# Layer scale on one core: laying rows out in HBM in contiguous blocks of 4, 60 and 64 per partition

## The chip, the core and the metric

The kernel runs on one core of a Trainium2 chip. The metric is the device time of one execution in microseconds; the median of three runs stands for a kernel. A profile is one more execution, recorded by the hardware profiler.

## What is computed

```python
B, S, D = 1024, 16, 512
# x, y: (B, S, D) bf16; gamma: (D,) bf16
def reference(x, y, gamma):
    return x + gamma * y
```

There are 1024 x 16 = 16384 rows of 512 values. A row is 1 KB in bf16. Each of x, y and the output has 16.78 MB, so 50.33 MB cross between HBM and SBUF. Every row is treated alike, so it does not matter to the result which row lies in which SBUF partition, as long as x, y and the output use one and the same assignment.

## The kernel before

**Layout.** The 16384 rows are spread over 128 partitions, 128 rows each. In HBM a partition's 128 rows are neighbours (`"(p n) d -> p n d"`, L52 to L54), so row r of one partition lies 128 KB from row r of the next. All of y stays in SBUF (`y_sb`, 128 rows of each partition). `x_sb` has room for 75 rows only: the second half of x is loaded over rows that have been used. The output is computed in place in `y_sb`.

**Transfers.** Two lists say what each DMA queue issues and in which order. `SP` (L10) has six loads, each written as (tensor, first row, end row) and for x also the row of `x_sb` where it goes: y rows 0 to 4, y 4 to 64, x 0 to 64, y 64 to 128, x 64 to 117, x 117 to 128. `ACT` (L11) has gamma and two stores, rows 0 to 64 and 64 to 128. The function `ring` walks such a list: y loads are issued at L116, x loads at L113, stores at L119, gamma at L110. `EARLY = (2, 0)` puts the first two loads of SP ahead of the barrier at the program's beginning. A transfer of r rows is moved as 128 packets of r KB, one for each partition, which the 16 DMA engines share, eight each.

**Waits.** A load of x into occupied rows waits for the additions that used them (`frees`), a store for the additions of its rows, both through `s_add`. The first store also waits for `s_go`, which TensorE raises (L135 to L137) once x rows 64 to 117 have landed. Each load has its own semaphore, and VectorE takes it ahead of the first operation on these rows.

**Compute.** The rows of a partition are worked on in pieces of 53, 11, 53 and 11 rows (`PIECES`). `DVE` (L18) gives the order: multiply pieces 0 and 1 by gamma (L156), add x to them (L165), then the same for pieces 2 and 3. Gamma is spread over the partitions once, by a matmul with a row of ones (L130) and a copy (L132).

The lines that set the layout:

```python
xv = xf.rearrange("(p n) d -> p n d", p=P)
yv = yf.rearrange("(p n) d -> p n d", p=P)
ov = of.rearrange("(p n) d -> p n d", p=P)
```

Of the kernel before, what the change touches and what calls it, by code (L numbers as in the profile page):

```python
# [3 lines left out]


PIECES = [53, 11, 53, 11]

SP = [('y', 0, 4), ('y', 4, 64), ('x', 0, 64, 0), ('y', 64, 128), ('x', 64, 117, 0), ('x', 117, 128, 64)]  # L10
ACT = [('g',), ('s', 0, 64), ('s', 64, 128)]  # L11

EARLY = (2, 0)


RELEASE = ('x', 64, 117, 0)

DVE = [('m', 0), ('m', 1), ('a', 0), ('a', 1), ('m', 2), ('m', 3), ('a', 2), ('a', 3)]  # L18
MULT, ADD = mybir.AluOpType.mult, mybir.AluOpType.add


def _take(sem, n, eng):


    return eng.wait_ge(sem, n).then_inc(sem, -n)  # L25


def kernel(
# [10 lines left out]
    P = nc.NUM_PARTITIONS  # L39
# [3 lines left out]
    xf = x.flatten_outer_dims()  # L43
    yf = y.flatten_outer_dims()
    of = out.flatten_outer_dims()
    N, D = xf.shape
    rows = N // P
    n = len(PIECES)
    assert sum(PIECES) == rows
    starts = [sum(PIECES[:c]) for c in range(n + 1)]  # L50
    dt = xf.dtype
    xv = xf.rearrange("(p n) d -> p n d", p=P)  # L52
    yv = yf.rearrange("(p n) d -> p n d", p=P)
    ov = of.rearrange("(p n) d -> p n d", p=P)  # L54

    gamma_row = nc.alloc_sbuf_tensor("gamma_row", [1, D], dt).ap()
    ones_row = nc.alloc_sbuf_tensor("ones_row", [1, P], dt).ap()
# [1 line left out]
    y_sb = nc.alloc_sbuf_tensor("y_sb", [P, rows, D], dt).ap()  # L59
    x_loads = [w for w in SP + ACT if w[0] == "x"]  # L60
    y_loads = [w for w in SP + ACT if w[0] == "y"]
    stores = [w for w in SP + ACT if w[0] == "s"]
    for loads in (x_loads, y_loads, stores):
# [7 lines left out]
    s_load = {w: sem("s_" + "_".join(map(str, w[:2]))) for w in x_loads + y_loads}  # L71
    s_add, s_go, s_rel, s_end, s_out = sem("s_add"), sem("s_go"), sem("s_rel"), sem("s_end"), sem("s_out")
    added = [a for kind, *a in DVE if kind == "a"]
    order = {a[0]: k for k, a in enumerate(added)}

    def meets(a, b, c, d):
        return a < d and c < b

    def pieces_of(a, b):
        return [c for c in range(n) if meets(starts[c], starts[c + 1], a, b)]  # L80

    def x_at(row):
        return next(w[3] + row - w[1] for w in x_loads if w[1] <= row < w[2])

    def frees(w):

        c = set()
        for v in x_loads[: x_loads.index(w)]:
            lo, hi = max(v[3], w[3]), min(v[3] + v[2] - v[1], w[3] + w[2] - w[1])
            if lo < hi:  # L90
                c |= set(pieces_of(v[1] + lo - v[3], v[1] + hi - v[3]))
        return sorted(c)
# [3 lines left out]
    def ring(eng, what, n_early):  # L96

        known, went = 0, False
        for k, w in enumerate(what):
            kind = w[0]  # L100
            need = frees(w) if kind == "x" else pieces_of(w[1], w[2]) + list(w[3:]) if kind == "s" else []
            need = max((order[c] + 1 for c in need), default=0)
            if kind == "s" and not went:
                _take(s_go, 1, eng)
                went = True
            if need > known:
                eng.wait_ge(s_add, need)
                known = need
            if kind == "g":
                i = eng.dma_start(out=gamma_row, in_=gamma.unsqueeze(0)).then_inc(s_gamma, 16)  # L110
            elif kind == "x":
                to = x_sb[:, w[3] : w[3] + w[2] - w[1], :]
                i = eng.dma_start(out=to, in_=xv[:, w[1] : w[2], :]).then_inc(s_load[w], 16)  # L113
            elif kind == "y":
                r = slice(w[1], w[2])
                i = eng.dma_start(out=y_sb[:, r, :], in_=yv[:, r, :]).then_inc(s_load[w], 16)  # L116
            else:
                r = slice(w[1], w[2])
                i = eng.dma_start(out=ov[:, r, :], in_=y_sb[:, r, :]).then_inc(s_out, 16)  # L119
            if k < n_early:  # L120
                early.append(i.ins)

    ring(nc.sync, SP, EARLY[0])
    ring(nc.scalar, ACT, EARLY[1])


# [7 lines left out]

    _take(s_load[RELEASE], 16, nc.tensor)  # L135
    nc.tensor.sem_inc(s_go, 1)
# [4 lines left out]
    def need(loads, c):  # L141
        for w in loads:
            if w not in landed and meets(starts[c], starts[c + 1], w[1], w[2]):
                if w == RELEASE:
                    _take(s_rel, 1, nc.vector)
                else:
                    _take(s_load[w], 16, nc.vector)
                landed.add(w)

    for kind, *args in DVE:  # L150
        c = args[0]
        yt = y_sb[:, starts[c] : starts[c + 1], :]
        if kind == "m":
            need(y_loads, c)
            g = gamma_sb[:, None, :].to_broadcast([P, PIECES[c], D])
            nc.vector.tensor_tensor(out=yt, in0=yt, in1=g, op=MULT).then_inc(s_dve, 1)  # L156
            open_mults += 1
        else:
# [4 lines left out]
            at = x_at(starts[c])  # L163
            xt = x_sb[:, at : at + PIECES[c], :]
            nc.vector.tensor_tensor(out=yt, in0=xt, in1=yt, op=ADD).then_inc(s_add, 1)  # L165
# [44 lines left out]
```

## Time and profile before

| what | value |
|---|---|
| median of 3 runs | 119.99 us (119.95 to 120.16) |
| span of the profiled execution | 118.7 us |
| own time of the profiled execution | not given apart from its span; the median run is 1.29 us above that span |
| VectorE busy | 70.0 us (59%), 10 instructions |
| TensorE busy | 0.6 us, 1 matmul |
| loads, SP's queue (q1) | 864 packets, 33.55 MB, 66.0% of 16 engines' span |
| stores and gamma, ACT's queue (q10) | 290 packets, 16.78 MB, 32.6% |
| one large multiplication or addition (53 rows) | 14.29 us |
| one small one (11 rows) | 3.08 us |

The span runs from the first recorded instruction to the last event of the kernel. Busy times are sums over an engine's instructions. For the queues, the share is the time that their packets took, as a part of 16 engines over the whole span; the two shares together are 98.6%. A packet count includes one small completion write for each DMA engine and transfer.

### The profile page before, as it was taken

How to read it: one execution, taken by the hardware profiler on the slowest of the kernel's cores; microseconds unless marked ns; L12 is line 12 of the kernel's file. 1: busy time of each engine (PE TensorE's matmuls, PEld its weight loads, DVE VectorE, ACT ScalarE, POOL GpSimd, SP SyncE). 2: the span in 40 equal slices, each digit the busy share in tenths (PEclk: the TensorE clock that was granted, in tenths of full speed). 3: DMA queues.
4: the chain of work that ended last, by engine and by line, in shares of the span. 5: the costliest groups of instructions: out<-in, count | busy, mean ns of one | idle time of the engine just before them, and what ended most of it. 6: DMA issues, size and time to landing. Idle time of an engine off the chain costs nothing. (4 is left out here: it accounts for less than half of the span.)

```text
span 118.7 us, 80 instructions
## 1 busy us (share of the span) xinstructions
PE 0.6 (0%) x1; PEld 0.1 (0%) x1; DVE 70.0 (59%) x10; POOL 0.2 (0%) x4
## 2 busy tenths in 40 slices
PE   0001000000000000000000000000000000000000
PEld 0000000000000000000000000000000000000000
DVE  0002000599999299999759999999999910000000
POOL 0000000000000000000000000000000000000000
DMA  8977977998899888998896969498899889988891
GB/s 268 571 332 331 663 331 331 596 464 353 353 486 574 353 353 353 640 420 353 353 585 293 585 293 585 205 634 353 353 596 464 353 353 420 640 353 353 353 663 44
DMA packets 1154, 50.33 MB, mean 424 GB/s; under 512 B 129, under 2 KB 130, under 8 KB 258
## 3 DMA queue, kind: packets, MB, share of 16 engines
q1 hardware_dynamic: 864, 33.55, 66.0%
q10 hardware_dynamic: 290, 16.78, 32.6%
HBM read 33.56 MB, written 16.78 MB: 424 GB/s over the span
## 5 line engine op out<-in xcount | busy, mean ns | idle before, releaser
L156 DVE TENSOR_TENSOR y_sb<-y_sb,gamma_sb 128x27136 bf16<-128x27136 bf16 (+1 forms) x4 | 34.6, 8688 | 12.3 <-DVEq L25 12.3
L165 DVE TENSOR_TENSOR y_sb<-x_sb,y_sb 128x27136 bf16<-128x27136 bf16 (+1 forms) x4 | 34.6, 8689 | 2.3 <-DVEq L25 2.2
L132 DVE CAST gamma_sb<-gamma_ps 128x512 bf16<-128x512 f32 x1 | 0.7, 692 | 8.8 <-DVEq L25 8.8
L127 DVE MEMSET ones_row<- 1x128 bf16 x1 | 0.2, 165 | 2.0 <-PEq L41 2.0
L130 PE MATMUL gamma_ps<-gamma_row,ones_row 1*128 1x512 bf16 x1 | 0.6, 577 | 10.2 <-PEq L25 10.2
L130 PEld LDWEIGHTS gamma_ps<-gamma_row,ones_row 1*128 1x128 bf16 x1 | 0.1, 99 | 10.2 <-issue 10.2
L194 POOL MEMSET const-bfloat16-1.0<- 128x1 bf16 x1 | 0.1, 101 | 0.0
L194 POOL MEMSET const-uint8-127<- 128x1 uint8 x1 | 0.1, 101 | 0.0
L194 POOL MEMSET const-float32-0.0<- 128x1 f32 x1 | 0.1, 98 | 0.2 <-issue 0.2
L194 POOL MEMSET const-float32-1.0<- 128x1 f32 x1 | 0.1, 98 | 0.0
## 6 DMA issues: line engine op xcount, KB each, us to landing
y_sb<-in_y_dram SPq DMA_DIRECT2D x1, 7680.0 KB, 21.4
x_sb<-in_x_dram SPq DMA_DIRECT2D x1, 6784.0 KB, 20.8
x_sb<-in_x_dram SPq DMA_DIRECT2D x1, 1408.0 KB, 23.8
y_sb<-in_y_dram SPq DMA_DIRECT2D x1, 512.0 KB, 3.8
out_dram<-y_sb ACTq DMA_DIRECT2D x2, 22.8
x_sb<-in_x_dram SPq DMA_DIRECT2D x1, 39.3
gamma_row<-in_gamma_dram ACTq DMA_DIRECT2D x1, 1.0 KB
y_sb<-in_y_dram SPq DMA_DIRECT2D x1, 58.3
```

The costliest lines, as they stand in the source:

```text
L127: nc.vector.memset(ones_row, 1.0).then_inc(s_ones, 1)
L130: nc.tensor.matmul(gamma_ps, ones_row, gamma_row, start=True, stop=True).then_inc(s_ps, 1)
L132: nc.vector.tensor_copy(out=gamma_sb, in_=gamma_ps).then_inc(s_dve, 1)
L156: nc.vector.tensor_tensor(out=yt, in0=yt, in1=g, op=MULT).then_inc(s_dve, 1)
L165: nc.vector.tensor_tensor(out=yt, in0=xt, in1=yt, op=ADD).then_inc(s_add, 1)
L194: nc = _bacc.Bacc("TRN2", target_bir_lowering=False, num_devices=1)
```

## The change

The rows are assigned to partitions differently. The 128 rows of a partition are split into blocks of 4, 60 and 64 rows (`BLOCKS`). A block of all partitions together is one contiguous stretch of HBM, and inside it a partition has its 4, 60 or 64 rows as neighbours. A new function `rows_of` gives the piece of a block that a transfer moves; loads and stores use it in place of the three views. A transfer may not cross from one block into another, so x rows 0 to 64 are loaded as 0 to 4 and 4 to 64, and the store of rows 0 to 64 becomes two, rows 4 to 64 first and then rows 0 to 4. The places in SBUF, the pieces of VectorE and their order are kept; the first addition (piece 0, rows 0 to 53) now takes two semaphores of x instead of one.

```diff
+BLOCKS = [4, 60, 64]
+
 PIECES = [53, 11, 53, 11]
...
-SP = [('y', 0, 4), ('y', 4, 64), ('x', 0, 64, 0), ('y', 64, 128), ('x', 64, 117, 0), ('x', 117, 128, 64)]
-ACT = [('g',), ('s', 0, 64), ('s', 64, 128)]
+SP = [
+    ("y", 0, 4),
+    ("y", 4, 64),
+    ("x", 0, 4, 0),
+    ("x", 4, 64, 4),
+    ("y", 64, 128),
+    ("x", 64, 117, 0),
+    ("x", 117, 128, 64),
+]
+ACT = [("g",), ("s", 4, 64), ("s", 0, 4), ("s", 64, 128)]
...
-    xv = xf.rearrange("(p n) d -> p n d", p=P)
-    yv = yf.rearrange("(p n) d -> p n d", p=P)
-    ov = of.rearrange("(p n) d -> p n d", p=P)
+    edges = [sum(BLOCKS[:c]) for c in range(len(BLOCKS) + 1)]
+    assert edges[-1] == rows
+
+    def rows_of(t, a, b):
+
+        c = max(c for c in range(len(BLOCKS)) if edges[c] <= a)
+        assert b <= edges[c + 1]
+        block = t[P * edges[c] : P * edges[c + 1]].rearrange("(p n) d -> p n d", p=P)
+        return block[:, a - edges[c] : b - edges[c], :]
...
-                i = eng.dma_start(out=to, in_=xv[:, w[1] : w[2], :]).then_inc(s_load[w], 16)
+                i = eng.dma_start(out=to, in_=rows_of(xf, w[1], w[2])).then_inc(s_load[w], 16)
...
-                i = eng.dma_start(out=y_sb[:, r, :], in_=yv[:, r, :]).then_inc(s_load[w], 16)
+                i = eng.dma_start(out=y_sb[:, r, :], in_=rows_of(yf, w[1], w[2])).then_inc(s_load[w], 16)
...
-                i = eng.dma_start(out=ov[:, r, :], in_=y_sb[:, r, :]).then_inc(s_out, 16)
+                i = eng.dma_start(out=rows_of(of, w[1], w[2]), in_=y_sb[:, r, :]).then_inc(s_out, 16)
```

More of the change, by code (lines that the diff above doesn't have):

```diff
@@ L3 @@
 from concourse import mybir
+BLOCKS = [4, 60, 64]
 PIECES = [53, 11, 53, 11]
-SP = [('y', 0, 4), ('y', 4, 64), ('x', 0, 64, 0), ('y', 64, 128), ('x', 64, 117, 0), ('x', 117, 128, 64)]
-ACT = [('g',), ('s', 0, 64), ('s', 64, 128)]
+SP = [
[8 more added lines that the diff above has]
+ACT = [("g",), ("s", 4, 64), ("s", 0, 4), ("s", 64, 128)]
 EARLY = (2, 0)
-RELEASE = ('x', 64, 117, 0)
-DVE = [('m', 0), ('m', 1), ('a', 0), ('a', 1), ('m', 2), ('m', 3), ('a', 2), ('a', 3)]
+RELEASE = ("x", 64, 117, 0)
+DVE = [("m", 0), ("m", 1), ("a", 0), ("a", 1), ("m", 2), ("m", 3), ("a", 2), ("a", 3)]
 MULT, ADD = mybir.AluOpType.mult, mybir.AluOpType.add
```

## The prediction

> **What bounds the kernel now.** I read the page first for its busy rows, then its queues, then the DMA-issue timeline, then the DMA view of the first four microseconds. The rows of 40 slices:
>
> ```profile
> DVE  0002000599999299999759999999999910000000
> DMA  8977977998899888998896969498899889988891
> HBM read 33.56 MB, written 16.78 MB: 424 GB/s over the span
> ```
>
> The DMA engines are loaded from the first slice to the last, VectorE is done a fifth before the end, and 50.33 MB in 118.7 us is 424 GB/s. The stretches say whether that leaves anything:
>
> ```profile
> 1.00:2.50 1.50, 0.00 (x0) 0.00 (x0) 0.17 (x1) 0.00 (x0) 1.00 0.95 216
> 2.50:118.40 115.90, 0.58 (x1) 0.10 (x1) 69.87 (x9) 0.00 (x0) 1.00 1.00 431
> ```
>
> The last two columns are DMA share and GB/s: from 2.5 to 118.4 us the engines are busy all the time at 431 GB/s, and only the first 1.5 us of traffic runs at half of it. So the time is bytes over a fixed rate, plus what is lost at the start and at the end. The start, in slices of 0.1 us (a packet's bytes count where it begins):
>
> ```profile
> DMA  0000000000999003029487989599999999000000
> GB/s 0 0 0 0 0 0 0 0 0 0 287 164 205 0 0 41 0 123 328 205 328 328 369 369 492 246 451 1024 1516 2704 860 1884 1311 1843 0 0 0 0 0 0
> DMA packets 160, 1.51 MB, mean 377 GB/s; under 512 B 16, under 2 KB 16, under 8 KB 144
> ```
>
> Sixteen 4 KB packets begin between 1.0 and 1.3 us, and then hardly any begins for 0.5 us: the engines stand in their first packet of y rows 0 to 4. The packet records give the sizes: a 4 KB packet later takes 159 ns, but of the first 16 two take 0.20 and 0.26 us, two 0.33 and 0.55 us, and the other twelve 0.62 to 1.16 us. Over the 128 packets of this transfer the sum is 30.6 us instead of 128 x 0.159 = 20.4, so 10.3 us over 16 engines, **0.64 us each**. Engines never stop afterwards (16 packets in flight from 2.3 to 117.7 us), so what an engine loses here it still lacks at the end: the last packets end between 117.74 and 118.38 us. Chaining packets end to start, the engine that ends last is one whose first packet took 1.03 us, 0.87 too many. Last data 118.38, last completion 118.7.
>
> **What the Trainium skill says.** "DMA: Bandwidth & Descriptors", section "Bandwidth" (Where 436 GB/s comes from), puts the fabric's ceiling at 435.2 GB/s, 27.2 per engine. The trace agrees: the 64 KB packet takes 2.418 us, 27.1 GB/s, for reads and writes alike. A better HBM address order cannot make these packets faster. The same page, "Latency and other measured facts", reports that copies whose partitions lie a large power of two apart lose rate (207 GB/s at 512 KiB, 103 at 4 MiB, against 214), and infers channels shared by streams in lock step. Here partitions lie 128 KB apart, and full rate in the steady part shows no such loss; but engines that take every fourth partition (its section "The descriptor swizzle") start 512 KB apart and all at once, and the stall at 1.3 us could be that effect. No run here shows it yet. Its section "Why small descriptors are slow" names a fixed cost per packet of about 3 cycles; the trace has 4 ns, below.
>
> **The change part by part.** *Addresses.* Each of the three row blocks becomes one stretch of HBM: partitions lie 4, 60 or 64 KB apart instead of 128. SBUF places, shapes of the DVE instructions, bytes (50.33 MB) and the order of the loads stay. For large packets I take zero: all 64, 60 and 53 KB packets already run at 27.1 GB/s.
>
> *More transfers.* x rows 0 to 64 become 4 + 60 (one more issue on SP), and the store of rows 0 to 64 becomes 60 + 4 (one more on ACT). On each engine a split turns 8 packets of 64 KB into 8 of 60 and 8 of 4 KB and adds one completion write. Start to start, the trace has 2.414 us for 64 KB, 2.263 for 60 KB and 0.155 for 4 KB: 2.263 + 0.155 - 2.414 = 4 ns per pair, and 6 ns for the completion. By recorded durations it is 159 + 2267 - 2418 = 8 ns and 9 ns. So 8 x 4 + 6 = 38 ns or 8 x 8 + 9 = 73 ns per split, and for both **+0.08 to +0.15 us**, wholly on the path because the engines never idle.
>
> *The start.* The y rows 0 to 4 keep 128 packets of 4 KB, but neighbouring engines start 16 KB apart, not 512. If the stall has to do with addresses, some or all of it goes. Lower bound 0. Upper bound: without any excess the engines would end on average 118.03 (the mean of the 16 ends) - 0.64 = 117.39, and the latest perhaps half of the start's stagger (1.04 to 1.30 us) behind, 117.55: 118.38 - 117.55 = **0.83 us**. That two engines got through at once while the others queued speaks for contention and against a cold latency common to all. I take six tenths, 0.5 us. A loss here is not excluded by any row, but with neighbours already 512 KB apart I see no pattern that would be worse.
>
> *Issues, queues and waits, at nothing.* The DMA issues as they stand:
>
> ```profile
> 0.00 0.84 SPq L116 DMA_DIRECT2D y_sb<-in_y_dram  x2
> 1.90 0.33 SPq L113 DMA_DIRECT2D x_sb<-in_x_dram  x1
> 1.91 0.52 ACTq L110 DMA_DIRECT2D gamma_row<-in_gamma_dram  x1
> 2.28 0.51 SPq L116 DMA_DIRECT2D y_sb<-in_y_dram  x1
> 55.78 0.81 SPq L113 DMA_DIRECT2D x_sb<-in_x_dram  x2
> 76.95 18.85 ACTq L119 DMA_DIRECT2D out_dram<-y_sb  x2
> ```
>
> The extra x issue (0.33 to 0.44 us) pushes the load of y rows 64 to 128 from 2.28 to about 2.7 us; its first packet starts at 38.4 us, behind the others in the queue. The x load of rows 64 to 117 still waits for the same first addition (issued 55.78, first packet 59.72). The extra store issue (0.35 us) goes out at about 77.3, and the engines are full of loads to 79.1. The store of rows 64 to 128 is issued at 95.46 after the last addition, and its first packet starts at 98.42: of the 2.96 us about 1.04 are needed (issue to first packet at the start), so 1.9 are spare. The first addition gains a second wait, for x rows 4 to 64; the queue lands them 0.04 to 0.07 us later than the whole block did, and the eight vector operations behind it, with the stores that wait for them, have those 1.9 us. If that cover went, the last store would be late next.
>
> **Sum.** The span is 118.7 us, and the median run of 119.99 has 1.29 us around it, which I leave alone; the page gives no separate total of the profiled execution. 118.7 - 0.5 + 0.11 = 118.3, plus 1.29: **119.6 us**.
>
> **Rivals.**
> *The start is cold, whatever the addresses* (34 in 100): the first reads after idle engines wait for something that contiguous blocks don't touch. For it: no later first packet of a new tensor (x at 21.0 us, the stores at 79.1) takes over 28 ns extra, with the same partition pitch. Against it: the two quick engines. Then only the splits count: 119.99 + 0.08 to 0.15 = 120.07 to 120.14. That the change does nothing to the bandwidth it is named for is this case too.
> *Small pieces stall again* (22 in 100), the one on the slower side: the new 4 KB transfers of x (about 21 us) and out (about 98 us) are hit as y's is. Each engine serves its own 8 packets in order, so a stall there adds to the end. For it: the only 4 KB transfer that the trace has lost 0.64 us per engine, and two packets in its midst took 0.43 and 0.64 us. Against it: most of its later packets took 159 ns, and by then the engines are spread in time. At the full 0.64 twice: 119.99 + 0.11 + 1.28 = 121.4; at a tenth to a third of that, 120.25 to 120.5. It decides from about 0.07 us per transfer, where 0.11 + 2 x 0.07 passes the bound below. A contiguous pattern that costs the large packets would look alike: 0.2% of their rate is 0.24 us.
>
> **How the numbers follow.** A measurement of this kernel tells about 0.2%, 0.24 us, from no change. A gain at the start of 0.35 to 0.83 us, less the splits, gives 119.25 to 119.75 and has 44 in 100: faster. The cold start, or a gain too small to show, gives 119.76 to 120.2, 34 in 100: no difference. Stalls or a worse pattern: 22 in 100, slower. The range 119.25 to 120.45 covers the first two and the mild half of the third; cases of both signs share the chance, so the likeliest case's own range, 119.25 to 119.75, is to be read beside it.
>
> **What would show it.** The view of the first four microseconds: if I am right, the hole between 1.3 and 1.8 us is filled, the stretch 1.0 to 2.5 us moves well over 216 GB/s, and y rows 0 to 4 land in under 3.5 us instead of 3.8. q1 should show 1008 packets (864 + 128 + 16) and q10 434 (290 + 128 + 16). The large packets should stay at 2.27 and 2.42 us and the new 4 KB ones at 0.16. I am wrong if the hole stays (then 120.1), or if it is filled and the last data still come at 118.4: then the engines' ends are set elsewhere.

## The result, and the profile after

The change makes the kernel slower: median 120.52 us (120.23 to 121.17, 6 runs) against 120.00 (119.95 to 120.16, 6 runs), ratio 1.0046 with a 95% interval of 1.0026 to 1.0066. The forecast was 119.6. The profiled execution itself took 121.17 us (span 119.8); it is the slowest of the six, so its numbers show the loss large. The same kernel run again beside other kernels gave 1.0028 (1.0012 to 1.0044), and there the profiled execution took 120.19. The two together bracket the usual case.

The page of the changed kernel, rows of 40 slices and queues:

```profile
DVE  0002000799999299999579999999999800000000
DMA  9879977999799889988999999799999989989990
q1 hardware_dynamic: 1008, 33.55, 65.7%
q10 hardware_dynamic: 434, 16.78, 32.4%
HBM read 33.56 MB, written 16.78 MB: 420 GB/s over the span
```

The shape is the same: DMA from the first slice to the last, VectorE far from it. The packet counts are the 1008 and 434 of the prediction. The issues of the x loads on SP, and of the stores on ACT, in its timeline (start, length, queue, line):

```profile
1.90 0.81 SPq L128 DMA_DIRECT2D x_sb<-in_x_dram  x2
2.77 0.42 SPq L131 DMA_DIRECT2D y_sb<-in_y_dram  x1
55.73 0.81 SPq L128 DMA_DIRECT2D x_sb<-in_x_dram  x2
76.88 18.90 ACTq L134 DMA_DIRECT2D out_dram<-y_sb  x3
```

They stand within 0.1 us of the old ones where they have a counterpart, except y rows 64 to 128 at 2.77, as worked out; VectorE's waits changed by little (the longest growth is before its first addition, 2.30 us instead of 2.17, as the multiplications ahead of it began 0.18 us earlier). The start did get better. The first four microseconds, in slices of 0.1 us, and then the two stretches of before (last column GB/s):

```profile
DMA  0000000000925739679999699799909000000000
GB/s 0 0 0 0 0 0 0 0 0 0 369 82 164 164 82 246 246 328 492 369 410 410 246 410 532 328 2130 6185 1270 0 614 0 0 0 0 0 0 0 0 0
```

```profile
1.00:2.50 1.50, 0.00 (x0) 0.00 (x0) 0.17 (x1) 0.00 (x0) 1.00 0.99 303
2.50:118.40 115.90, 0.58 (x1) 0.10 (x1) 69.86 (x9) 0.00 (x0) 1.00 1.00 430
```

The hole from 1.3 to 1.8 us is filled, and the first stretch moves 303 GB/s instead of 216. But 2.5 to 118.4 us is not faster for it, and the span goes on to 119.8. Where the time goes shows in two lines of the list of DMA issues (KB, then us from issue to landing), before and then after:

```profile
x_sb<-in_x_dram SPq DMA_DIRECT2D x1, 1408.0 KB, 23.8
y_sb<-in_y_dram SPq DMA_DIRECT2D x1, 512.0 KB, 3.8
```

```profile
x_sb<-in_x_dram SPq DMA_DIRECT2D x1, 1408.0 KB, 25.0
y_sb<-in_y_dram SPq DMA_DIRECT2D x1, 512.0 KB, 3.4
```

The first y piece lands 0.4 us earlier; the last x load, rows 117 to 128, lands 1.2 us later after its issue. In stretches of two microseconds around it, before and then after:

```profile
76.00:78.00 2.00, 0.00 (x0) 0.00 (x0) 1.99 (x1) 0.00 (x0) 1.00 0.99 422
78.00:80.00 2.00, 0.00 (x0) 0.00 (x0) 1.87 (x1) 0.00 (x0) 1.00 1.77 761
```

```profile
76.00:78.00 2.00, 0.00 (x0) 0.00 (x0) 1.97 (x1) 0.00 (x0) 1.00 1.11 383
78.00:80.00 2.00, 0.00 (x0) 0.00 (x0) 1.88 (x1) 0.00 (x0) 1.00 1.49 639
```

(A packet counts in the stretch where it begins, so a stretch can pass the real rate: at 78 to 80 us the first large store packets begin.) The DMA share is high and the bytes are fewer: packets are in progress but take longer. The packet records say which. An 11 KB packet of x rows 117 to 128 usually takes 0.42 us; in the changed kernel 33 of the 128 are over 30 ns longer (before: 2), the longest takes 1.28 us, and the excess is 6.9 us in all, 0.43 per engine. These 33 all begin between 76.1 and 78.6 us, before the first store packet at 79.2, so it is not reads against writes.

A transfer has 128 packets and 16 completions, one for each engine, and what an engine loses it does not make up: in one kernel below, where a packet stalls at the very start, the latest engine is 0.91 us behind the mean at the end of each of the first six loads, from 21 to 77 us. The completion records give the mean and the latest engine at the end of each load (us from the first recorded instruction):

| all data landed, us | before: mean, latest | after: mean, latest | after, run again |
|---|---|---|---|
| y 0 to 4 | 3.44, 3.76 | 3.12, 3.36 | 2.93, 3.16 |
| y 4 to 64 | 21.58, 21.86 | 21.44, 21.68 | 21.35, 21.58 |
| x 0 to 64 | 40.93, 41.21 | 40.90, 41.16 | 40.78, 41.01 |
| y 64 to 128 | 60.28, 60.56 | 60.25, 60.54 | 60.13, 60.36 |
| x 64 to 117 | 76.33, 76.60 | 76.28, 76.53 | 76.18, 76.39 |
| x 117 to 128 | 79.71, 79.99 | 80.03, 81.09 | 79.68, 80.10 |
| last store | 118.34, 118.67 | 118.72, 119.82 | 118.37, 118.83 |

This table is the story. Of the 0.4 to 0.6 us won at the start, half is gone after the next load, most by the end of the first x rows in the one execution, and then x rows 117 to 128 cost the latest engine 1.16 us more than before (in the repeat 0.32).

### The profile page after: what moved, and what is told of

It reads as the page before. It is cut to its first block, busy times and chain, and to the rows that moved or that the text cites. A ratio compares the mean times of both kernels' runs of the same rounds, so it can differ in the third digit from the quotient of the medians.

```text
span 119.8 us, 83 instructions
## 1 busy us (share of the span) xinstructions
PE 0.6 (0%) x1; PEld 0.1 (0%) x1; DVE 70.0 (58%) x10; POOL 0.2 (0%) x4
## 2 busy tenths in 40 slices
DMA packets 1442, 50.33 MB, mean 420 GB/s; under 512 B 161, under 2 KB 162, under 8 KB 546
## 3 DMA queue, kind: packets, MB, share of 16 engines
q1 hardware_dynamic: 1008, 33.55, 65.7%
```

## Experiments

Three theories were put up first. **A**: the 11 KB pieces of x, now 64 KB apart, are read slowly. **B**: the extra transfers cost the time. **C**: the 60 KB packets are slow in their new places. Later ones replace them. Each kernel was timed beside the kernel before, whose median lay between 119.90 and 120.07 us from set to set, so the ratios are to be compared rather than the times. The table collects all kernels. "Excess" is the time of the packets over the usual one for their size (0.159, 0.272, 0.422, 2.004, 2.267, 2.418 us for 4, 7, 11, 53, 60, 64 KB), over 16 engines: at the start (packets begun before 4 us), in the rest of the first 64 rows, and in the loads of rows 64 to 128. "Lag" is the latest engine's end minus the mean end. Excess, mean end and lag come from one execution each, ratios from the timed runs. "After, run again" above is "after again" here.

| kernel | ratio to before (95%) | start | rows 0-64 | rows 64-128 | mean end | lag |
|---|---|---|---|---|---|---|
| before | 1 | 0.66 | 0.02 | 0.07 | 118.34 | 0.33 |
| after | 1.0046 (1.0026, 1.0066) | 0.54 | 0.15 | 0.46 | 118.72 | 1.09 |
| after again | 1.0028 (1.0012, 1.0044) | 0.23 | 0.17 | 0.28 | 118.37 | 0.46 |
| splits only, 128 | 1.0005 (0.9994, 1.0016) | 0.60 | 0.02 | 0.03 | 118.39 | 0.41 |
| 64, 64 | 1.0048 (1.0034, 1.0062) | 0.71 | 0.18 | 0.17 | 118.75 | 1.00 |
| 4, 124 | 1.0031 (1.0018, 1.0044) | 0.34 | 0.15 | 0.08 | 118.28 | 0.77 |
| 4, 60, 53, 11 | 1.0008 (1.0000, 1.0016) | 0.43 | 0.05 | 0.06 | 118.24 | 0.28 |
| after, y split too | 1.0043 (1.0027, 1.0059) | 0.27 | 0.12 | 0.40 | 118.64 | 0.56 |
| before, y split too | 1.0005 (0.9996, 1.0014) | 0.56 | 0.04 | 0.05 | 118.33 | 0.36 |
| after, 11 rows first | 1.0015 (1.0003, 1.0026) | 0.51 | 0.03 | 0.18 | 118.42 | 0.40 |
| before, no 4-row piece | 1.0002 (0.9992, 1.0012) | 0.71 | 0.02 | 0.27 | 118.48 | 0.26 |
| 124, 4 | 0.9999 (0.9988, 1.0010) | 0.44 | 0.04 | 0.05 | 118.28 | 0.29 |
| 64, 64, no 4-row piece | 1.0036 (1.0026, 1.0047) | 0.70 | 0.02 | 0.23 | 118.47 | 0.67 |
| 64, 53, 11 | 1.0016 (1.0009, 1.0022) | 0.67 | 0.02 | 0.03 | 118.41 | 0.32 |
| 4, 124, first loads swapped | 1.0070 (1.0058, 1.0082) | 0.73 | 0.01 | 0.08 | 118.50 | 1.03 |
| after, first loads swapped | 1.0077 (1.0062, 1.0092) | 0.71 | 0.01 | 0.29 | 118.72 | 0.60 |
| 117, 11 | 1.0000 (0.9992, 1.0007) | 0.55 | 0.02 | 0.03 | 118.30 | 0.43 |

**The splits alone.** The new lists on the old addresses:

```diff
-BLOCKS = [4, 60, 64]
+BLOCKS = [128]
```

> The new transfer lists (x rows 0 to 4 and 4 to 64, stores 4 to 64 and 0 to 4) on the old layout, partitions 128 KB apart. Theory A (the loss sits in the 11 KB packets of x rows 117 to 128, which the new layout puts 64 KB apart per partition): those packets stay at 0.42 us with under 0.05 us per engine of excess, and the time is that of before plus the splits' 0.08 to 0.15 us: 120.05 to 120.2. Theory B (the extra transfers themselves cost the time): 120.4 to 120.6 as in the changed kernel. Theory C (the 60 KB packets in their new places): as A here.

Measured: 1.0005, that is +0.06 us (-0.07 to +0.19). All the 4 KB packets in mid-stream took their 0.159 us, excess 0.00. B falls; the cost of the splits fits what was worked out, though by the times alone it cannot be told from none.

**Two halves.** Contiguous blocks without any extra transfer:

```diff
-BLOCKS = [4, 60, 64]
+BLOCKS = [64, 64]
```

with the transfer lists of the kernel before.

> The old lists on a layout of two contiguous blocks of 64 rows per partition: no extra transfer, but x rows 117 to 128 are 11 KB pieces 64 KB apart, as in the changed kernel, and y rows 0 to 4 are 4 KB pieces 64 KB apart. Theory A: the 11 KB packets have 0.2 to 0.6 us per engine of excess and the time is 120.3 to 120.8. Theory B: 119.9 to 120.1. Theory C: 119.9 to 120.1, as no block has 60 rows.

Measured: 1.0048, as slow as the full change. The 11 KB packets have 0.16 us per engine, a little under what A said, and the 60 KB packets, now 60 of every 64 KB, have 0.17 after the start that none of the three theories had.

**Only the 4-row block contiguous.**

```diff
-BLOCKS = [4, 60, 64]
+BLOCKS = [4, 124]
```

> The changed kernel with the blocks 4 and 124 instead of 4, 60 and 64: the 4-row piece stays contiguous, all other partitions are 124 KB apart. Theory A: the 11 KB packets are quick again, the start keeps its small gain (about 0.1 us per engine), the splits cost about 0.1: 119.9 to 120.1. Theory B: 120.4 to 120.6. Theory C: 119.9 to 120.1, and the 60 KB packets are back at 2.267 us with no excess.

Measured: 1.0031, 120.39 us, with runs from 119.9 to 121.22. The 11 KB packets are quick (0.01 us per engine) as A says, yet the time is not. The 60 KB packets have the excess, and after y rows 4 to 64 the latest engine is 0.41 us behind the mean, where it was 0.18 after y rows 0 to 4. A is not the whole, and C, which had these packets quick here, falls.

**The tail as a block of its own.**

```diff
-BLOCKS = [4, 60, 64]
+BLOCKS = [4, 60, 53, 11]
...
     ("x", 4, 64, 4),
-    ("y", 64, 128),
+    ("y", 64, 117),
+    ("y", 117, 128),
...
-ACT = [("g",), ("s", 4, 64), ("s", 0, 4), ("s", 64, 128)]
+ACT = [("g",), ("s", 4, 64), ("s", 0, 4), ("s", 64, 117), ("s", 117, 128)]
```

> The changed kernel with the last block of 64 rows divided into contiguous blocks of 53 and 11, so that the 11 KB pieces lie 11 KB apart; y rows and the store of 64 to 128 are each split into two transfers to match. Theory A: the excess of the 11 KB packets falls to under 0.1 us per engine; two more splits cost 0.08 to 0.15 us; 120.1 to 120.3. Theory B: slower than the changed kernel, 120.7 to 121.1. Theory C: 120.5 or more, with the excess in the 60 KB packets.

Measured: 1.0008, with four transfers more than the kernel before. Its last x load, from the list of DMA issues:

```profile
x_sb<-in_x_dram SPq DMA_DIRECT2D x1, 1408.0 KB, 23.9
```

23.9 against 25.0 in the changed kernel. Most of the loss is gone, although two splits were added, so most of it does sit in how the 64-row block is read.

**A second 11 KB load, and its control.**

```diff
-    ("y", 64, 128),
+    ("y", 64, 117),
+    ("y", 117, 128),
```

in the changed kernel, and the same on the kernel before.

> The changed kernel with y rows 64 to 128 loaded as 64 to 117 and 117 to 128: a second load of 11 KB pieces 64 KB apart, in mid-queue. Theory A (11 KB pieces 64 KB apart are read slowly by some engines, and what an engine loses it keeps): the excess comes twice, the latest engine falls 0.3 to 1 us further behind, and the time is 120.8 to 121.5. Theory D (only the last load is slow, because the loads end there): one more split of about 0.05 us, so 120.5 to 120.7, and the y packets at 0.42 us.

> The same split of y rows 64 to 128 on the kernel before, where the pieces lie 128 KB apart: the control. Theories A and D alike: the 11 KB packets at 0.42 us, one split of 0.04 to 0.07 us, 120.0 to 120.1.

Measured: 1.0043 (120.62 us) and 1.0005. The control is as expected within the noise. In the changed layout A misses. D has the time and the quick y pieces, but not its mechanism, since the last load is quick too: all 256 11 KB packets are (0.01 us per engine), and the 53 KB packets have 0.40, nearly all in packets that end between 44 and 52 us, in y rows 64 to 117. So it is not the 11 KB piece as such that is slow; some part of the 64-row block is, and which part is hit changes.

**The eleven rows at the block's beginning.**

```diff
-PIECES = [53, 11, 53, 11]
+PIECES = [53, 11, 11, 53]
...
-    ("x", 64, 117, 0),
-    ("x", 117, 128, 64),
+    ("x", 75, 128, 0),
+    ("x", 64, 75, 64),
...
-RELEASE = ("x", 64, 117, 0)
+RELEASE = ("x", 75, 128, 0)
...
-DVE = [("m", 0), ("m", 1), ("a", 0), ("a", 1), ("m", 2), ("m", 3), ("a", 2), ("a", 3)]
+DVE = [("m", 0), ("m", 1), ("a", 0), ("a", 1), ("m", 3), ("m", 2), ("a", 3), ("a", 2)]
```

> The changed kernel with the 11-row piece of x at the beginning of its block of 64 rows (rows 64 to 75, loaded last; rows 75 to 128 ahead of it; vector pieces 53, 11, 11, 53 in the matching order): same size, same 64 KB between partitions, other place inside the 64 KB. Theory A (the distance makes it): the excess stays, 120.3 to 120.8. Theory A2 (the place of the eleven rows, at the end of each 64 KB, makes it): the 11 KB packets are quick and the time is 119.9 to 120.2.

Measured: 1.0015 (120.20 us), at the upper end of A2's range. The 11 KB packets are quick (0.015 us per engine), as A2 says, but the 53 KB ones have 0.16, most of it between 64 and 72 us, which neither theory had.

**No small packets at the start.**

```diff
-SP = [('y', 0, 4), ('y', 4, 64), ...
+SP = [('y', 0, 64), ...
```

on the kernel before.

> The kernel before with y rows 0 to 64 loaded as one transfer of 64 KB pieces instead of 4 and 60: no small packets at the start. If the stall of the first reads belongs to the many small packets, the engines' ends draw together and the time falls to 119.4 to 119.7 (0.3 to 0.5 us of stall and one split of 0.05 us less). If the first read of each engine stalls whatever its size, 119.9 to 120.0, the split alone.

Measured: 1.0002, so the time did not fall. The start in slices of 0.1 us:

```profile
DMA  0000000000999009900000000000000000000009
GB/s 0 0 0 0 0 0 0 0 0 0 5243 3277 655 0 0 655 655 0 0 0 0 0 0 0 0 0 0 0 0 0 0 0 0 0 0 0 0 0 0 655
```

Sixteen 64 KB packets begin and nothing follows for over two microseconds. They take 0.36 to 0.91 us more than usual, 11.3 us in all, about what the 4 KB packets lost together (10.3). So the stall belongs to the first reads of an engine, not to small packets. This kernel is also the one in which the old layout shows an excess in the 53 KB packets (0.20), without a growing lag (0.26).

At this point two things could be told apart: **F**, reads of only a part of a contiguous block (53 or 11 of every 64 KB) are held up, and **W**, any large load of the new layouts is; and for blocks 4 and 124, **G**, the even start brings engines in step and some fall behind in the next load, and **P**, the distance of 124 KB does it.

**The changed kernel again**, with no edit.

> The changed kernel once more, beside the others on one chip. Theory F (reads that take only part of a contiguous block, 53 or 11 of every 64 KB, are held up): 120.3 to 120.7 and the excess again in the loads of x rows 64 to 128. Theory W (engines that read in step collide at times, in any large load of the new layouts; which load is hit changes from execution to execution): the same time, but the excess may lie in other loads.

Measured: 1.0028. The excess is again in the loads of x rows 64 to 128, 0.09 in the 53 KB and 0.19 in the 11 KB packets. The 60 KB packets of the first half have 0.17, though each of these loads takes a whole block. The line of the last x load:

```profile
x_sb<-in_x_dram SPq DMA_DIRECT2D x1, 1408.0 KB, 24.2
```

**Blocks 124 and 4.**

```diff
-BLOCKS = [4, 60, 64]
+BLOCKS = [124, 4]
...
-    ("x", 0, 4, 0),
-    ("x", 4, 64, 4),
-    ("y", 64, 128),
+    ("x", 0, 64, 0),
+    ("y", 64, 124),
+    ("y", 124, 128),
     ("x", 64, 117, 0),
-    ("x", 117, 128, 64),
+    ("x", 117, 124, 64),
+    ("x", 124, 128, 71),
 ]
-ACT = [("g",), ("s", 4, 64), ("s", 0, 4), ("s", 64, 128)]
+ACT = [("g",), ("s", 0, 64), ("s", 64, 124), ("s", 124, 128)]
```

> Blocks of 124 and 4 rows instead of 4 and 124: partitions are again 124 KB apart, but the first load, y rows 0 to 4, is not contiguous, so the start is as in the kernel before. Three extra transfers (y, x, store), some 0.12 to 0.2 us. Theory G (a quick, even start leaves the engines in step, and then they collide): no excess in the large packets, 120.1 to 120.2. Theory P (124 KB apart is what holds them up): 0.1 to 0.2 us per engine of excess in the 60 KB packets as with blocks 4 and 124, and 120.3 to 120.7.

Measured: 0.9999, that is -0.01 us (-0.14 to 0.12), so the three extra transfers do not show. The 60 KB packets after the start have 0.06 us per engine and the lag is 0.29. That speaks against P; G stands.

**Whole blocks in the first half, and everywhere.**

```diff
-BLOCKS = [4, 60, 64]
+BLOCKS = [64, 64]        # second kernel: [64, 53, 11]
...
-SP = [('y', 0, 4), ('y', 4, 64), ...
+SP = [('y', 0, 64), ...  # second kernel: also y 64 to 117 and 117 to 128, and their stores
```

(the `SP` and `ACT` of the kernel before otherwise).

> Two contiguous blocks of 64 rows with y rows 0 to 64 in one transfer: in the first half every load now takes a whole block, in the second x is still taken as 53 and 11 of each 64 KB. Theory F: no excess in the first half after the first packets, some (0.1 to 0.4 us per engine) in x rows 64 to 128: 120.1 to 120.5. Theory W: as the halves with the 4-row piece, 120.4 to 120.7, with excess in the first half too.

> Blocks of 64, 53 and 11 rows, y rows 0 to 64 in one transfer, y rows 64 to 128 and their store split in 53 and 11: every transfer takes a whole contiguous block, and there is no 4-row piece. One store more than in the kernel before and as many loads, some 0.04 to 0.07 us. Theory F: no excess after the first packets and the engines' ends within 0.6 us: 119.9 to 120.1, the best layout of the set. Theory W: 120.3 to 120.7.

Measured: 1.0036 and 1.0016. Read as whole blocks, the first half loses its excess (0.02 against 0.18 with blocks 64 and 64 and the 4-row piece; the start is another one too), while x rows 117 to 128 of the 64-row block keep theirs (0.18 in the 11 KB packets). With every load a whole block, both halves are clean (0.02 and 0.03) and the lag is back to 0.32. The last x load, first and second kernel:

```profile
x_sb<-in_x_dram SPq DMA_DIRECT2D x1, 1408.0 KB, 24.4
x_sb<-in_x_dram SPq DMA_DIRECT2D x1, 1408.0 KB, 23.9
```

These two start alike (0.70 and 0.67), so the second half is a plain comparison, and it is F, packet by packet. The time is only in part: the second kernel is still 0.19 us slower than before by its ratio (0.11 to 0.26), where its one extra transfer was priced at 0.04 to 0.07, and so not the best of the set, as F had it. The rest is not explained by its profile.

**The first two loads swapped**, with all addresses kept, for blocks 4 and 124 and in the changed kernel:

```diff
-    ("y", 0, 4),
     ("y", 4, 64),
+    ("y", 0, 4),
```

> The kernel with blocks of 4 and 124 rows and one edit: y rows 4 to 64 are loaded ahead of y rows 0 to 4. Every address and every packet is the same, only the even start of the 4-row piece is gone: the first packets are of 60 KB. Theory G (the quick start brings the engines in step, and a few fall behind in the 60 KB packets that follow): no further excess in the 60 KB packets once each engine's first is through, engines' ends within 0.6 us, 120.0 to 120.15. Theory P (the addresses do it): ends 0.8 us or more apart and 120.3 to 120.7, as with the 4-row piece first.

> The same swap in the changed kernel with blocks 4, 60 and 64. Theory G with F: the first half is clean, what is left is the excess in x rows 64 to 128 (0.1 to 0.4 us per engine, in the 53 or 11 KB packets), 120.2 to 120.5. Theory P with F: no change against the changed kernel, 120.4 to 120.6, with excess in the 60 KB packets.

Measured: 1.0070 and 1.0077, slower than all others. The 60 KB packets after the first ones are clean in both (0.01 us per engine), at the very addresses that had 0.15 to 0.17 with the 4-row piece first: so that part of the excess hangs on the start, not on the addresses, as G says. That the engines then run in step, which is G's reason for it, no run shows. The times went against both expectations, and the start shows why in the profiled execution. First four microseconds of blocks 4 and 124, swapped:

```profile
DMA  0000000009999900090000000000000000000009
GB/s 0 0 0 0 0 0 0 0 0 1229 1843 2458 3072 614 0 0 0 614 0 0 0 0 0 0 0 0 0 0 0 0 0 0 0 0 0 0 0 0 0 3686
```

Sixteen packets of 60 KB begin before 1.8 us. Fifteen take 2.27 to 3.29 us, one takes 3.86, that is 1.59 too many. Its engine is the latest ever after: 0.91 us behind the mean when y rows 4 to 64 have landed, 1.03 at the end. The last packets of the same execution, 114 to 119.6 us in slices of 0.14:

```profile
DMA  0090000000999090000900000000000000000000
GB/s 0 0 468 0 0 0 0 0 0 0 3745 936 1872 0 468 0 0 0 0 468 0 0 0 0 0 0 0 0 0 0 0 0 0 0 0 0 0 0 0 0
```

Fifteen engines begin their last 64 KB packet between 115.4 and 116.1 us, and one at 116.8. Nearly all of the lag at the end comes from a single packet's stall at 1 us. In the changed kernel, swapped, the lag is 0.61 us after the first load and 0.60 at the end, and the excess of rows 64 to 128 is left (0.17 in the 53 KB and 0.12 in the 11 KB packets), as F says.

**Neither cause.**

```diff
-BLOCKS = [4, 60, 64]
+BLOCKS = [117, 11]
```

with y rows 0 to 4 and 4 to 64 first, x rows 0 to 64 in one transfer, and y rows 64 to 128 and their store split in 53 and 11.

> Blocks of 117 and 11 rows, the old 4 and 60 rows of y first and x rows 0 to 64 in one transfer; y rows 64 to 128 and their store split in 53 and 11: two extra transfers, 0.08 to 0.15 us. The 11 KB pieces lie contiguously, everything else 117 KB apart, no piece 64 KB apart and no contiguous first load. Theory F: no excess in the 11 and 53 KB packets. If an uneven distance already shortens the start (0.44 us per engine with 124 KB against 0.66 with 128), 119.85 to 120.0; if not, 120.0 to 120.2.

Measured: 1.0000 (0.9992 to 1.0007), no excess in the 11 and 53 KB packets (0.01 us or less in each load), start 0.55. These parts of a 117-row block are read cleanly, so F is shown for the 64-row block only. No version of the set is measurably faster than the kernel before.

## Why the prediction was wrong

**The step that failed is "for large packets I take zero".** That the old addresses ran at the engines' full 27.1 GB/s was read as room on the HBM side for any order of addresses, and it is not; and the 11 KB packets, where the profiled execution lost most, stood in no term at all. Reads that take 53 or 11 (or 60) of every 64 KB of a contiguous block had 0.16 to 0.43 us of excess per engine in all seven profiles with such a block; 64 KB packets that take the whole block had 0.03 at most after the first ones. Of the eight profiles with 117, 124 or 128 KB between partitions, seven had 0.03 to 0.08 in rows 64 to 128 and one 0.27. Read in whole blocks of 53 and 11, these rows bring the kernel from 1.0046 to 1.0008, so about 0.45 us hang on the 64-row block (0.24 by the repeat's 1.0028). The usual packet did stay at 2.27 and 2.42 us, as the prediction asked; the loss sits in a minority of slow packets, which that sign does not see. In the prediction this case stood as one sentence, at the end of the rival on small pieces ("a contiguous pattern that costs the large packets would look alike"), inside the 22 in 100 for slower, and deserved a price of its own. Writes never showed an excess (0.01 us per engine or less in every kernel), but no store here takes a part of a 64-row block, so that case was not tried.

**The start: right in kind, wrong in worth.** The hole was filled, and the y piece landed 0.4 us earlier for the latest engine (0.6 in the repeat), near the 0.5 that I took. But 0.22 and 0.32 of it were given back by the end of the next load. Even with rows 64 to 128 read cleanly (blocks 4, 60, 53, 11), the kernel is 0.10 us slower than before (0.00 to 0.19) and not 0.4 faster. So about half of the 0.92 us between the forecast of 119.6 and the measured 120.52 is the gain at the start that did not come through to the end; this is an estimate from the ratios, with the two further splits of this kernel in it. The kernels with swapped loads show, in one profile each, that the loss in the next load follows the even start: with it the 60 KB packets have 0.12 to 0.17 us in four profiles, in the swapped kernels 0.01. (Blocks 4, 60, 53, 11 and the kernel with eleven rows first had the even start and only 0.03 to 0.05: this part changes from execution to execution.) The reading of the cause was too narrow as well: kernels whose first packets are of 60 or 64 KB lose the same 0.7 us at their first reads, whether this load is one contiguous stretch (blocks of 60 or 64 rows) or not. Only a contiguous load of 4 KB packets lost less (0.10 to 0.39, against 0.41 to 0.68 where they lie 64 to 128 KB apart).

The prediction named this sign of being wrong, the hole filled and the last data no earlier, and it came: the last data land at 119.47 us in the profiled execution and at 118.48 in the repeat, against 118.34 before. (The prediction's times of packets lie 0.04 us later than the trace's. Half of the stagger of 0.26 us added to 117.39 is 117.52, so its upper bound for the gain is 0.86 us and not 0.83; nothing rests on either.)

**The splits: right in size, as far as can be told.** 0.08 to 0.15 us forecast, 0.06 (-0.07 to 0.19) measured. In the kernel with the splits alone, x rows 0 to 64 take 19.43 us from the mean completion of the load before to their own, against 19.35 in one transfer: 0.076 us for one split, just above the 0.038 to 0.073 that were worked out. The rival *small pieces stall again* was wrong in its mechanism though right in its sign: the 4 KB packets of x and out had no excess at all. The rival *cold start* was wrong in the number, and the stall did shrink.

**Issues, queues and waits at nothing: right.** VectorE's last addition ends at 95.4 us in both kernels, and the last store is issued at 95.44 (before: 95.46).

**"What an engine loses here it still lacks at the end": right, and it is the main point.** I used it for the gain and priced everything else per engine on average. The end is the latest engine's: in the profiled execution of the change the mean end moved by 0.39 us, the latest by 1.15.

What stays open: why parts of a 64 KB block are read more slowly than parts of a 117, 124 or 128 KB one, and which load is hit when. No kernel here takes parts of a block at another distance below 117 KB, so whether 64 KB as such matters or any short distance is not shown. Nor was it measured how addresses are spread inside the HBM. The kernel before without the 4-row piece had 0.20 us in its 53 KB packets too, so the old addresses are less prone to it, not free of it. The packet records name no engine, so whether the same engines are hit each time is not known.

## What to carry to other kernels

When 16 engines each have a fixed share of every transfer, a kernel at the DMA limit ends with its slowest engine: compare the mean and the latest completion of each transfer, load by load, and not the mean rate alone. Before a new HBM layout is called free because the packets already run at full rate, look at what each transfer then takes of a block: whole blocks of 11, 53 and 64 rows had 0.04 us of excess at most here once the first packets were through (whole blocks of 60 rows up to 0.17 after the even start), parts of a 64-row block 0.16 to 0.43. A gain at the start counts only if it is still there at the last completion.

## What was not expected of the hardware

- At their first reads the engines lose about the same on average: 0.41 to 0.68 us per engine with 4 KB packets 64, 117, 124 or 128 KB apart, and 0.67 to 0.73 with 60 or 64 KB packets. A contiguous 512 KB of 4 KB packets as first load brought it to 0.10 to 0.39, or 0.23 to 0.54 with the first packets of the next load.
- One packet out of 1442 with 1.59 us of stall at the start left the latest engine 0.91 us behind the mean until 77 us; at the end the lag was 1.03 us, about that of the changed kernel's profile (1.09).
- A 4 KB packet in mid-stream costs next to nothing beyond its bytes: 0.155 us from start to start, against 0.151 for the same bytes inside a 64 KB packet.
